# Windowed attention scored in blocks of 32 queries with 96 keys instead of 64 queries with 128 keys

## The chip, the cores and the metric

The kernel runs on one core of a Trainium2 chip. The time is the device time of one execution in microseconds (us); the runs shown are three executions of the same program, given by their median. A profile is one further execution, recorded by the hardware profiler. The engines are PE (TensorE: matmuls; PEld is its weight load), DVE (VectorE), ACT (ScalarE), POOL (GpSimd) and SP (SyncE, which here issues all DMAs).

## The reference

Sliding-window attention, then a feed-forward block with a short convolution and a gate, all in float32:

```python
B, H, S, D = 8, 8, 576, 64                      # batch, heads, sequence, head dimension
scores = q @ k.T / 8
rel = pos[:, None] - pos[None, :]
scores = where((rel >= 0) & (rel < 64), scores, -1e9)   # a query sees itself and the 63 keys before it
attn = softmax(scores); x = attn @ v            # heads laid side by side: x is [8, 576, 512]
h = relu(x @ w_in)                              # w_in 512 x 1024
conv[s] = cw[0]*h[s-1] + cw[1]*h[s] + cw[2]*h[s+1]      # zero outside the sequence
out = (h * sigmoid(conv)) @ w_out               # w_out 1024 x 512
```

## The kernel before

The 8 x 576 positions are cut into `NU` = 12 units of `NX` = 384 positions, each of `NT` = 6 tiles of `W` = 64 queries. A tile of 64 queries needs 128 keys (its own 64 and the 64 before); the first tile of a sequence has only its own 64 keys and is called narrow here (`keys_of`).

Attention of a unit is made in four batches `b` = 0..3. A batch is three tiles of four heads (two heads stand in the two halves of the 128 rows, `h`; two head pairs in the two halves of the columns, `p`). A batch passes these steps, and each is one entry of a plan:

- `qk` (L260, PE): twelve matmuls, in array tiles of 64 rows x 64 columns, write the scores into the two PSUM tiles `sc`. All batches use the same two `sc` tiles.
- `row_max` (L268, DVE): six instructions add the mask, write the scores to `s` and their row extremes to `nm`.
- `exps` (L278, ACT): six exponentials, which also sum up their rows. `reciprocal` (L281, L282, DVE).
- `normalise` (L286): scales the whole batch, on DVE in units 0 to 2, on POOL from unit 3 on.
- Transposition of the probabilities to `ub`, keys in rows: in units 0 and 1 (`BY_PE`) by PE (`transpose_pe`, L292) with a copy on ACT (`untile`, L297); from unit 2 on by DVE (`transpose`, L302), whose 32 x 32 blocks SP then puts in place by DMA (`place`, L313).

`values` (L362, PE) multiplies by v, and ACT and DVE split the result into a rounded part `xh` and a rest `xl` (L366, L369). `mm1` (L382) and `mm2` (L445) are the two large products, each as three matmuls on such split operands. Between them stand ReLU (ACT), the convolution (ACT, and DVE's L416 twice per column block), sigmoid (ACT), the gate (L428, DVE) and the split of the gated values (L432 ACT, L436 DVE).

The weights arrive as 64-bit words and are turned into float32 in the first part of the run, in sixteen pieces (eight of w_in, then eight of w_out): per piece ACT, POOL (L201), DVE (L202, L204), ACT, DVE (L208), then POOL rounds it (L217) and DVE writes the rest (L218, into `wil` or `wol`). `mm1` of column block f needs piece f of w_in, `mm2` piece f of w_out.

The order of all this is not written by hand. Each step is an entry with an engine, an assumed cost, what it reads and writes, and a due time; `queued` plays the entries through once with the assumed costs and records which it would take next on each engine. Due times of the first units stand in the table `START` (loads, weight pieces, scores, exponentials, values); the later units use fixed due times. The chip then runs each engine's instructions in that recorded order, with waits on semaphores.

Of the kernel before, what the change touches and what calls it, by code (L numbers as in the profile page):

```python
# [16 lines left out]
W = 64  # L17
B, H, S, D = 8, 8, 576, 64
# [36 lines left out]
def queued(works):  # L55
# [28 lines left out]
    while left:  # L84
        best = None
        for e, ws in waiting.items():
            if not ws:
                continue
            start = max(free[e], min(x.ready for x in ws))
            if best is None or start < best[0]:  # L90
                best = (start, e)
        start, e = best
        x = min((x for x in waiting[e] if x.ready <= start),
                key=lambda x: x.t - (0.5 if x.kind and x.kind == state[e] else 0.0))
        waiting[e].remove(x)
        turn = SWITCH[e] if e in SWITCH and (x.kind != state[e] if e == "PE" else x.kind and x.kind != state[e]) else 0.0
        if e == "PE" or x.kind:
            state[e] = x.kind
        end = free[e] = start + turn + x.cost
        if x.mb:  # L100
            dma = max(dma, end) + x.mb * 4.1
            end = dma + 1.9
        order.append(x)
        left -= 1
        for y in x.after:
            y.needs -= 1
            y.ready = max(y.ready, end + (0.0 if e == "PE" else 0.06) if y.eng == e else end + 0.2)
            if y.needs == 0:
                waiting[y.eng].append(y)
# [5 lines left out]
    "v0": -32.34,  # L115
    "pv0": -6.2,
    "conv": -32.87,
    "bits": (-33.3, -36.61, -40.93, -30.92),
    "qk1": -17.78,
    "v1": 0.96,  # L120
    "qk2": 4.55,
    "qk0": (-43.65, -39.69, -27.02, -34.75),
    "ex0": (-23.8, -21.02, -18.17, -16.66),
    "sc1": (-5.0, -10.37, -7.03, -0.86),
    "ex1": (0.34, 1.83, 2.14, 4.14),
    "in": (-23.25, -22.61, -8.35, -8.05, -5.93, -4.59, -3.56, -0.9),
    "out": (0.44, 1.55, 5.22, 5.44, 6.56, 8.03, 8.94, 11.09),
    "pv": ((4.73, 5.71, 6.92, 7.43), (5.83, 6.08, 6.48, 6.89)),
    "ex": ((5.79, 8.44, 8.97, 9.87), (6.28, 7.38, 9.35, 9.93)),
# [5 lines left out]
def attention_moe(ctx: ExitStack, tc: tile.TileContext, q, k, v, w_in, conv_w, w_out, out):  # L135
# [15 lines left out]
    mask = pool.tile([P, P], F32, name="mask")  # L151
# [4 lines left out]
    ss = many(4, [P, NB, 2, P], F32, "s")  # L156
# [38 lines left out]
    def to_f32(t, n, st, x, kb, kt):  # L195

        lw, hw, xu = st[..., 0], st[..., 1], x.bitcast(U32)
        s = n / DM

        at(t, "ACT", 0.6 * s + 0.05, lambda: nc.scalar.activation(x, hw.bitcast(F32), AF.Abs), r=[kb], w=[kt])  # L200
        at(t, "POOL", 1.45 * s + 0.15, lambda: nc.gpsimd.tensor_scalar(x, x, TINY, None, op0=ALU.max), w=[kt])  # L201
        at(t, "DVE", 0.37 * s + 0.06, lambda: nc.vector.tensor_scalar(  # L202
            xu, xu, 3, 0x3FFFFFF8, op0=ALU.logical_shift_left, op1=ALU.bitwise_and), w=[kt])
        at(t, "DVE", 0.61 * s + 0.06, lambda: nc.vector.scalar_tensor_tensor(  # L204
            xu, hw, 0xC0000000, xu, op0=ALU.bitwise_and, op1=ALU.bitwise_or), r=[kb], w=[kt])
# [27 lines left out]

    def make_masks():
        nc.gpsimd.memset(mask, 0.0)
        for h in range(2):
            mh = mask[h * W:(h + 1) * W]

            nc.gpsimd.affine_select(out=mh, in_=mh, compare_op=ALU.is_gt, fill=MASKED,
                                    base=0, pattern=[[1, P]], channel_multiplier=-1)  # L240

            nc.gpsimd.affine_select(out=mh, in_=mh, compare_op=ALU.is_ge, fill=MASKED,
                                    base=W, pattern=[[-1, P]], channel_multiplier=1)
        make_identity(nc, ident)

    def keys_of(u, t):
        return W if (u * NT + t) % SB == 0 else P  # L250

    def qk(u, b):
        g, t0 = b // 2, b % 2 * NB
        for i in range(NB):
            t = t0 + i
            n = keys_of(u, t)
            for h in range(2):
                hs = slice(h * D, (h + 1) * D)
                for p in range(2):
                    nc.tensor.matmul(sc[h][p * W:(p + 1) * W, (i + 1) * P - n:(i + 1) * P],  # L260
                                     qs[hs, 2 * g + p, t * W:(t + 1) * W],
                                     ks[hs, 2 * g + p, t * W + P - n:t * W + P], start=True, stop=True)

    def row_max(u, b):
        for i in range(NB):
            n = keys_of(u, b % 2 * NB + i)
            for h in range(2):
                nc.vector.tensor_tensor_reduce(  # L268
                    out=ss[b][:, i, h, P - n:], in0=sc[h][:, (i + 1) * P - n:(i + 1) * P], in1=mask[:, P - n:],
# [3 lines left out]
    def exps(u, b, i):  # L273
        n = keys_of(u, b % 2 * NB + i)
        for h in range(2):
            e = slice(2 * i + h, 2 * i + h + 1)
            x = ss[b][:, i, h, P - n:]
# [6 lines left out]
    def normalise(b, on):  # L284
        sv = ss[b].rearrange("p t h k -> p (t h) k")
        on.tensor_tensor(sv, sv, rs[b].unsqueeze(2).broadcast_to([P, 2 * NB, P]), ALU.mult)  # L286
# [3 lines left out]
    def transpose_pe(b, j):  # L290
        for i in range(NB):
            nc.tensor.transpose(po[b % 2 * 2 + j][:, i * P:(i + 1) * P],  # L292
                                ss[b].rearrange("p t h k -> p (t h) k")[:, NB * j + i], ident)
# [6 lines left out]
    def transpose(b):  # L300
        o = b % 2 * 2 * NB
        nc.vector.transpose(  # L302
            tbuf[:, b // 2, :, o:o + 2 * NB, :].rearrange("p j t q -> p t j q"),
            ss[b].rearrange("p t h (j q) -> p (t h) j q", q=32))
# [6 lines left out]
    def place(g, i):  # L311
        for j in range(i % 2, i % 2 + 3):
            nc.sync.dma_start(ub[g][32 * j:32 * j + 32, i], tbuf[32 * i:32 * i + 32, g, j])  # L313

    def softmax(u, qk_at, ex_at):
        for b in range(4):
            g, t = b // 2, qk_at[b]
            at(t, "PE", 0.70, lambda b=b: qk(u, b), r=[("k", g), ("q", g)], w=["sc", ("turn", b)], kind="tiled")
            for i in range(NB):
                if keys_of(u, b % 2 * NB + i) < P:  # L320
                    at(t + 0.1, "POOL", 0.2, lambda b=b, i=i: nc.gpsimd.memset(ss[b][:, i, :, :W], 0.0), w=[("s", b, i)])
            at(t + 0.17, "DVE", 1.27, lambda b=b: row_max(u, b), r=["sc", "mask"],
               w=[("s", b, i) for i in range(NB)] + [("nm", b)])
            t = ex_at[b]
            for i in range(NB):
                at(t, "ACT", 0.8, lambda b=b, i=i: exps(u, b, i), r=[("nm", b)],
# [3 lines left out]
            if u < 3:  # L330
                at(t, "DVE", 0.9, lambda b=b: normalise(b, nc.vector), r=[("r", b)], w=[("s", b, i) for i in range(NB)])
            else:
                at(t, "POOL", 1.5, lambda b=b: normalise(b, nc.gpsimd), r=[("r", b)], w=[("s", b, i) for i in range(NB)])
            t += 0.4
            sr = [("s", b, i) for i in range(NB)]
            if u < BY_PE:
                for j in range(2):
                    m = ("po", b % 2 * 2 + j)
                    at(t, "PE", 0.6, lambda b=b, j=j: transpose_pe(b, j), r=sr + ["mask"], w=[m])
                    at(t + 0.1, "ACT", 0.45, lambda b=b, j=j: untile(b, j), r=[m], w=[("u", g, i) for i in range(4)])  # L340
            else:
                t = max(t, when[-1][2] + 0.1)
                at(t, "DVE", 0.9, lambda b=b: transpose(b), r=sr, w=[("T", g)] + [("bits", i) for i in T_BITS[g]])
# [142 lines left out]
    at(-99, "POOL", 3.0, make_masks, w=["mask"])  # L486
# [111 lines left out]
```

## Time and profile before

| | |
|---|---|
| Runs shown | 543.62, 543.86, 543.85 us; median 543.85 |
| Profiled execution | 543.88 us, of which the span from first to last instruction is 542.1 |
| PE busy / PE weight loads | 510.9 us (94%) / 483.0 us (89%) |
| DVE, ACT, POOL busy | 405.6 (75%), 390.6 (72%), 122.9 us (23%) |
| Chain that ended last | PE 83%, DVE 14%, rest 3% |

How to read it: the busy shares are means over a first part, in which weights are converted and the first units' attention is made, and a long later part. The row of forty slices (13.55 us each) parts them. A matmul's recorded duration covers its way through the array, so two that follow each other overlap; the distance of their starts is what each costs. The distances below are of that kind.

### The profile page before, as it was taken

To read this page: it belongs to the slowest core of one execution; us is meant where nothing else is said; L and a number is where in the kernel's file an instruction comes from. 1 tells how busy PE (TensorE), PEld (TensorE's weight loads), DVE (VectorE), ACT (ScalarE), POOL (GpSimd) and SP (SyncE) were. 2 spreads that over 40 slices of the span, in tenths; PEclk is the share of its full clock that TensorE was granted. 3 is DMA by queue.
4 is the path that set the end of the run, shared out by engine and by line. 5 is a ranking of instruction groups with operands and counts; after the bars stand their busy time and mean duration, and the time that the engine had idled before them with its cause. 6 is when DMAs were issued, how large, how long until landed. Compare 5 with 4: busy or idle time off the path is not lost.

```text
span 542.1 us, 12584 instructions
## 1 busy us (share of the span) xinstructions
PE 510.9 (94%) x4656; PEld 483.0 (89%) x4656; DVE 405.6 (75%) x1151; ACT 390.6 (72%) x1030; POOL 122.9 (23%) x200
## 2 busy tenths in 40 slices
PE   3697598999999999999999999999999999999997
PEld 2576487999999999999999999999999999999997
DVE  2999999987767778678669677677679578575552
ACT  5798886975885885785986785786885786864441
POOL 3544665302220211212211211202211202200000
PEclk9999799999999999999999999999999999999999
DMA  8764254146154254463255262362344452030011
GB/s 337 267 255 182 91 190 160 38 130 242 27 176 136 79 140 127 137 202 108 70 173 177 57 209 53 123 171 86 129 126 125 142 160 85 19 103 2 1 58 60
DMA packets 27709, 69.83 MB, mean 129 GB/s; under 512 B 5632, under 2 KB 15360, under 8 KB 27648
## 3 DMA queue, kind: packets, MB, share of 16 engines
q1 hardware_dynamic: 27648, 69.03, 39.5%
q8 instruction: 37, 0.61, 0.5%
q14 instruction: 24, 0.20, 0.1%
HBM read 47.73 MB, written 9.47 MB: 106 GB/s over the span
## 4 chain that ended last, share of the span: by engine, by line
PE 83%; DVE 14%; issue 1%; DMA 1%; ACT 0%; SPq 0%; DVEq 0%
PE po L445 36%; PE acc L382 34%; PE sc L260 6%; PE acc L362 6%; DVE s L268 2%; DVE c L416 2%; DVE w L208 2%; DVE s L286 1%; DVE w L204 1%; DVE w L202 1%; DVE wil L218 1%; DVE wol L218 1%; DMA q<-in_q_dram 1%; DVE xl L369 1%; DVE gl L436 1%
## 5 line engine op out<-in xcount | busy, mean ns | idle before, releaser
L382 PE MATMUL acc<-xh,wih 128*128 128x384 f32 x384 | 132.7, 346 | 9.1 <-ACT hbuf L403 6.9
L445 PE MATMUL po<-gh,woh 128*128 128x386 f32 (+1 forms) x384 | 132.5, 345 | 0.4 <-POOL woh L217 0.4
L416 DVE SCALAR_TENSOR_TENSOR c<-hbuf,cw,c 128x386 f32<-128x386 f32 (+1 forms) x192 | 123.9, 693 | 10.9 <-ACT c L409 10.8
L445 PE MATMUL po<-gh,wol 128*128 128x386 f32 (+1 forms) x384 | 129.8, 338 | 1.2 <-DVE wol L218 1.2
L382 PE MATMUL acc<-xh,wil 128*128 128x384 f32 x384 | 130.5, 340 | 0.5 <-DVE wil L218 0.5
L382 PE MATMUL acc<-xl,wih 128*128 128x384 f32 x384 | 130.5, 340 | 0.0
L445 PE MATMUL po<-gl,woh 128*128 128x386 f32 (+1 forms) x384 | 129.8, 338 | 0.0
L278 ACT ACTIVATE s<-s,nm 128x128 f32<-128x128 f32 (+1 forms) x288 | 110.1, 384 | 5.6 <-DVE nm L268 5.3
L268 DVE CUSTOM_DVE_ANT_0 s<-sc,mask 128x128 f32<-128x128 f32 (+1 forms) x288 | 62.2, 277 | 33.2 <-PE sc L260 33.0
L382 PEld LDWEIGHTS acc<-xh,wih 128*128 128x128 f32 x384 | 72.7, 189 | 13.0 <-POOL w L201 7.1
L286 POOL TENSOR_TENSOR s<-s,r 128x768 f32<-128x768 f32 x36 | 54.1, 1504 | 98.2 <-DVE r L282 85.4
L445 PEld LDWEIGHTS po<-gh,woh 128*128 128x128 f32 x384 | 72.3, 188 | 4.5 <-issue 3.4
L445 PEld LDWEIGHTS po<-gh,wol 128*128 128x128 f32 x384 | 72.3, 188 | 1.8 <-DVE wol L218 1.8
L382 PEld LDWEIGHTS acc<-xh,wil 128*128 128x128 f32 x384 | 72.8, 189 | 0.8 <-DVE wil L218 0.8
L382 PEld LDWEIGHTS acc<-xl,wih 128*128 128x128 f32 x384 | 72.7, 189 | 0.0
L445 PEld LDWEIGHTS po<-gl,woh 128*128 128x128 f32 x384 | 72.3, 188 | 0.0
L436 DVE TENSOR_TENSOR gl<-c,gh 128x772 fp32r<-128x772 f32 (+1 forms) x48 | 46.0, 959 | 33.4 <-ACT gh L432 33.3
L403 ACT ACTIVATE hbuf<-acc 128x384 f32<-128x384 f32 x64 | 30.9, 486 | 45.2 <-PE acc L382 44.7
L428 DVE TENSOR_TENSOR c<-c,hbuf 128x772 f32<-128x772 f32 (+1 forms) x48 | 45.9, 956 | 22.3 <-ACT c L423 22.2
L392 POOL COPY hbuf<-hbuf 128x4 f32<-128x4 f32 x44 | 14.4, 327 | 212.5 <-DVE c L428 212.5
L423 ACT ACTIVATE c<-c 128x772 f32<-128x772 f32 (+1 forms) x48 | 40.7, 848 | 19.5 <-DVE c L416 19.2
L278 ACT ACTIVATION_READ_ACCUMULATOR s<-s,nm 128x1 f32 x288 | 54.1, 188 | 0.0
(56 smaller groups left out, 641.0 us busy)
## 6 DMA issues: line engine op xcount, KB each, us to landing
v<-in_v_dram SPq DMA_DIRECT2D x24, 768.0 KB, 4.8
ub<-T SPq DMA_DIRECT2D x240, 48.0 KB, 1.9
k<-in_k_dram SPq DMA_DIRECT2D x24, 448.0 KB, 5.5
q<-in_q_dram SPq DMA_DIRECT2D x24, 384.0 KB, 6.4
out_dram<-ot SPq DMA_DIRECT2D x8, 772.0 KB, 4.4
T<-in_w_in_dram SPq DMA_DIRECT2D x6, 512.0 KB, 6.3
T<-in_w_out_dram SPq DMA_DIRECT2D x6, 512.0 KB, 3.3
out_dram<-ot SPq DMA_DIRECT2D x3, 768.0 KB, 7.3
```

The costliest lines, as they stand in the source:

```text
L260: nc.tensor.matmul(sc[h][p * W:(p + 1) * W, (i + 1) * P - n:(i + 1) * P], qs[hs, 2 * g + p, t * W:(t + 1) * W], ks[hs, 2 * g + p, t * W + ...
L268: nc.vector.tensor_tensor_reduce(out=ss[b][:, i, h, P - n:], in0=sc[h][:, (i + 1) * P - n:(i + 1) * P], in1=mask[:, P - n:], scale=-0.125, ...
L278: nc.scalar.activation(x, x, AF.Exp, bias=nms[b][:, e], scale=-1.0, accum_out=sms[b][:, e])
L286: on.tensor_tensor(sv, sv, rs[b].unsqueeze(2).broadcast_to([P, 2 * NB, P]), ALU.mult)
L362: nc.tensor.matmul(acc[bank(("v", u, c))][h * D:(h + 1) * D, t * W:(t + 1) * W], vs[:, c, t, h], ub[g][:, 2 * p:2 * p + 2, 2 * t + h], sta ...
L382: nc.tensor.matmul(acc[bank(("m", u, f))][:, :NX], w[:, f, c], x[u % 2][:, c], start=(c == 0 and j == 0), stop=(c == NC - 1 and j == 2))
L403: nc.scalar.activation(hbuf[:, f, o:o + NX], ps[:, :NX], AF.Relu)
L416: nc.vector.scalar_tensor_tensor(c, hbuf[:, f, e:e + n], cw[:, e, f:f + 1], c, op0=ALU.mult, op1=ALU.add)
L423: nc.scalar.activation(c, c, AF.Sigmoid)
L428: nc.vector.tensor_tensor(c, c, hbuf[:, 2 * i:2 * i + 2, 1:1 + n], ALU.mult)
L436: nc.vector.tensor_tensor(gls[ring(u, i)][:, :, :n], cs[i % 2][:, :, :n], ghs[ring(u, i)][:, :, :n].bitcast(F32), ALU.subtract)
L445: nc.tensor.matmul(po[o][:, :n], w[:, f, es], x, start=(f == 0 and j == 0), stop=(f == NF - 1 and j == 2))
```

## The change

Queries are taken in blocks of `HW` = 32, each with its `KW` = 96 keys (its own 32 and the 64 before). A tile of 64 queries is two such blocks, in the two 32-row halves `s` of its 64 rows. What changes with that:

- `qk` makes 24 matmuls per batch instead of 12, in array tiles of 64 rows x 32 columns, each over 96 keys; there are no narrow tiles any more, since a second mask covers the keys before a sequence's start.
- `row_max`, `exps`, `normalise` and `transpose` work on 96 columns per tile and head instead of 128 (64 in narrow tiles). The buffers `s` are now windows in tiles `sp` that hold 32 zero columns between two blocks' probabilities; POOL writes these zeros once (`zero_pads`), and the memsets of narrow tiles (L321) go.
- `transpose_pe` becomes two ordinary matmuls with half of the identity (`iv`, 64 columns) for each former transpose, reading 128 columns of `sp` that are a block's 96 keys and 32 zeros.
- `place` issues the same twelve DMAs per half unit, at shifted offsets.
- `make_masks` issues 16 selects for two masks instead of 4 for one.
- Assumed costs and the due times in `START` are others, so the recorded order of the first units changes on every engine.

```diff
-    mask = pool.tile([P, P], F32, name="mask")
+    mask = many(2, [P, KW], F32, "mask")
-    ss = many(4, [P, NB, 2, P], F32, "s")
+    sp = many(4, [P, HW + 2 * NB * P], F32, "s")
+    ss = [x[:, HW:].rearrange("p (t h k) -> p t h k", t=NB, h=2)[:, :, :, :KW] for x in sp]
...
     def make_masks():
+        for first in range(2):
+            nc.gpsimd.memset(mask[first], 0.0)
+            for i in range(4):
+                mi = mask[first][i * HW:(i + 1) * HW]
+                nc.gpsimd.affine_select(out=mi, in_=mi, compare_op=ALU.is_gt, fill=MASKED,
+                                        base=0, pattern=[[1, KW]], channel_multiplier=-1)
+                nc.gpsimd.affine_select(out=mi, in_=mi, compare_op=ALU.is_ge, fill=MASKED,
+                                        base=W, pattern=[[-1, KW]], channel_multiplier=1)
+                if first:
+                    nc.gpsimd.memset(mi[:, :W - i % 2 * HW], MASKED)
         make_identity(nc, ident)
+    def zero_pads():
+        for x in sp:
+            nc.gpsimd.memset(x[:, :2 * NB * P].rearrange("p (e k) -> p e k", k=P)[:, :, :HW], 0.0)
+            nc.gpsimd.memset(x[:, 2 * NB * P:], 0.0)
...
     def qk(u, b):
-            t = t0 + i
-            n = keys_of(u, t)
-            for h in range(2):
-                hs = slice(h * D, (h + 1) * D)
-                for p in range(2):
-                    nc.tensor.matmul(sc[h][p * W:(p + 1) * W, (i + 1) * P - n:(i + 1) * P],
-                                     qs[hs, 2 * g + p, t * W:(t + 1) * W],
-                                     ks[hs, 2 * g + p, t * W + P - n:t * W + P], start=True, stop=True)
+            for p in range(2):
+                for s in range(2):
+                    r, t = p * W + s * HW, (t0 + i) * W + s * HW
+                    for h in range(2):
+                        hs = slice(h * D, (h + 1) * D)
+                        nc.tensor.matmul(sc[h][r:r + HW, i * KW:(i + 1) * KW], qs[hs, 2 * g + p, t:t + HW],
+                                         ks[hs, 2 * g + p, t:t + KW], start=True, stop=True)
...
     def transpose_pe(b, j):
+        iv = ident.rearrange("r (p s q) -> r s p q", s=2, q=HW)
         for i in range(NB):
-            nc.tensor.transpose(po[b % 2 * 2 + j][:, i * P:(i + 1) * P],
-                                ss[b].rearrange("p t h k -> p (t h) k")[:, NB * j + i], ident)
+            m = po[b % 2 * 2 + j][:, i * P:(i + 1) * P].rearrange("k (p s q) -> k s p q", s=2, q=HW)
+            for s in range(2):
+                o = (NB * j + i) * P + (1 - s) * HW
+                nc.tensor.matmul(m[:, s], sp[b][:, o:o + P], iv[:, s], start=True, stop=True)
...
-            dma = max(dma, end) + x.mb * 4.1
+            dma = max(dma, end) + x.mb * 2.6
-    "in": (-23.25, -22.61, -8.35, -8.05, -5.93, -4.59, -3.56, -0.9),
+    "in": (-33.517, -26.541, -25.396, -20.689, -14.772, -11.612, -10.617, -8.312),
-            at(t, "PE", 0.70, lambda b=b: qk(u, b), r=[("k", g), ("q", g)], w=["sc", ("turn", b)], kind="tiled")
+            at(t, "PE", 0.52, lambda b=b: qk(u, b), r=[("k", g), ("q", g)], w=["sc", ("turn", b)], kind="tiled")
-    at(-99, "POOL", 3.0, make_masks, w=["mask"])
+    at(-99, "POOL", 5.0, make_masks, w=["mask"])
+    at(-98, "POOL", 1.2, zero_pads, w=["pads"])
```

How the recorded order moves is seen best at three places. The first is SP's queue at the start of the program, before and then after (k, q and v are inputs, `T` and `ot` hold raw weight words, `cbits` the raw convolution weights):

```order
L183 DMA k<-in_k_dram 128x896
L184 DMA q<-in_q_dram 128x768
L183 DMA k<-in_k_dram 128x896
L184 DMA q<-in_q_dram 128x768
L214 DMA T<-in_w_in_dram 128x1024 x3
L229 DMA cbits<-in_conv_w_dram 128x48
```

```order
L218 DMA T<-in_w_in_dram 128x1024
L233 DMA cbits<-in_conv_w_dram 128x48
L187 DMA k<-in_k_dram 128x896
L188 DMA q<-in_q_dram 128x768
L187 DMA k<-in_k_dram 128x896
L188 DMA q<-in_q_dram 128x768
```

A weight piece and the small `cbits` now go out ahead of the first k and q.

The second is PE after the scores of unit 0, before and then after (`po` receives the transposes, `acc` the product with v):

```order
L292 MATMUL po_112<-ident,s_78 128x128 x3
L292 MATMUL po_113<-ident,s_78 128x128 x3
L292 MATMUL po_114<-ident,s_79 128x128 x3
L292 MATMUL po_115<-ident,s_79 128x128 x3
L362 MATMUL acc_110<-ub_61,v 64x64 x12
```

```order
L303 MATMUL po_113<-ident,s_79 128x2x32 x6
L303 MATMUL po_114<-ident,s_79 128x2x32 x6
L303 MATMUL po_115<-ident,s_80 128x2x32 x6
L303 MATMUL po_116<-ident,s_80 128x2x32 x6
```

The twelve transposes of two batches are 24 matmuls; behind them now stand the 24 score matmuls of a batch of unit 1, and only then the first product with v.

The third is DVE around the last weight piece, before and then after (`c` is the convolution, `gl` the rest of the gated values, `T` now holds transposed probabilities):

```order
L286 TENSOR_TENSOR s_81<-s_81,r_93 128x768
L208 ISA w_104<-ot,w_104 128x1024
L302 STREAM_TRANSPOSE T<-s_80 128x6x4x32
L428 TENSOR_TENSOR c_94<-c_94,hbuf 128x772
L218 TENSOR_TENSOR wol<-w_104,woh 128x512
L302 STREAM_TRANSPOSE T<-s_81 128x6x4x32
L436 TENSOR_TENSOR gl_100<-c_94,gh_97 128x772
```

```order
L293 TENSOR_TENSOR s_81<-s_81,r_93 128x6x96
L222 TENSOR_TENSOR wol<-w_105,woh 128x512
L312 STREAM_TRANSPOSE T<-s_81 128x6x3x32
L288 TENSOR_SCALAR sm_90<-sm_90 128x6
L289 RECIPROCAL r_94<-sm_90 128x6
L293 TENSOR_TENSOR s_82<-s_82,r_94 128x6x96
L436 TENSOR_TENSOR c_95<-c_95,hbuf 128x772
```

The last piece (`wol`) is now written before the last normalisation of unit 2, one transposition and the gate of the next column block, which stood ahead of it.

More of the change, by code (lines that the diff above doesn't have):

```diff
@@ L311, in place @@
     def place(g, i):
[L312 to L313 removed]
+        for j in range(3):
+            o = HW * (i % 2 + j)
+            nc.sync.dma_start(ub[g][o:o + HW, i], tbuf[HW * i:HW * (i + 1), g, j])
     def softmax(u, qk_at, ex_at):
@@ L317, in softmax @@
             g, t = b // 2, qk_at[b]
-            at(t, "PE", 0.70, lambda b=b: qk(u, b), r=[("k", g), ("q", g)], w=["sc", ("turn", b)], kind="tiled")
[L319 to L322, printed above, removed]
+            at(t, "PE", 0.52, lambda b=b: qk(u, b), r=[("k", g), ("q", g)], w=["sc", ("turn", b)], kind="tiled")
+            at(t + 0.17, "DVE", 1.1, lambda b=b: row_max(u, b), r=["sc", "mask"],
                w=[("s", b, i) for i in range(NB)] + [("nm", b)])
@@ L330, in softmax @@
             if u < 3:
-                at(t, "DVE", 0.9, lambda b=b: normalise(b, nc.vector), r=[("r", b)], w=[("s", b, i) for i in range(NB)])
+                at(t, "DVE", 0.72, lambda b=b: normalise(b, nc.vector), r=[("r", b)], w=[("s", b, i) for i in range(NB)])
             else:
-                at(t, "POOL", 1.5, lambda b=b: normalise(b, nc.gpsimd), r=[("r", b)], w=[("s", b, i) for i in range(NB)])
+                at(t, "POOL", 1.15, lambda b=b: normalise(b, nc.gpsimd), r=[("r", b)], w=[("s", b, i) for i in range(NB)])
             t += 0.4
```

60 lines of the change are left out of this document (26 added, 34 removed).

## The prediction

> **What bounds the kernel now.** I read the page first: its busy shares and forty slices.
>
> ```profile
> PE 510.9 (94%) x4656; PEld 483.0 (89%) x4656; DVE 405.6 (75%) x1151; ACT 390.6 (72%) x1030; POOL 122.9 (23%) x200
> PE   3697598999999999999999999999999999999997
> DVE  2999999987767778678669677677679578575552
> ```
>
> PE is full only from about the eighth slice on; before that DVE is. Next, the busy time by stretch (columns: length, then PE, PEld, DVE, ACT, POOL, PEclk, DMA):
>
> ```profile
> 0.00:22.00 22.00, 11.38 (x132) 8.76 (x132) 11.98 (x62) 13.48 (x52) 7.76 (x30) 1.00 0.87 336
> 22.00:97.60 75.60, 58.48 (x589) 52.10 (x589) 74.85 (x210) 63.12 (x171) 42.46 (x41) 0.95 0.47 168
> 97.60:520.00 422.40, 422.37 (x3830) 403.81 (x3831) 310.79 (x871) 307.61 (x800) 72.67 (x130) 1.00 0.38 116
> ```
>
> From 22 to 97.6 us DVE works 74.85 of 75.60 us and PE leaves 17.1 idle; from there PE has no hole at all. So the time is made of two things: when DVE has got through the weights and the first three units, and how much PE has to do from then on. The chain of waits says the same, and so does DVE's timeline at the last weight piece (last two rows), whose first reader, a block of L445, starts on PE right behind it:
>
> ```profile
> 94.82 0.87 DVE gl L436
> 95.69 1.28 DVE s L286
> 96.98 0.61 DVE wol L218
> 97.63 2.20 PE po L445 x11
> ...
> 107.16 0.68 DVE L218 TENSOR_TENSOR wol<-w,woh 128x512 fp32r<-128x512 f32 x1
> 108.11 0.34 PE L445 MATMUL po<-gh,woh 128*128 128x386 f32 x1
> ```
>
> I use that last piece as the mark, 107.8 us. The profiled execution took 543.88 us, 1.8 more than its span of 542.1, and stands at the median of the runs shown (543.85).
>
> **Scores on PE, after the mark.** A full batch, a narrow one, and what follows each:
>
> ```profile
> 144.22 0.89 PE L260 MATMUL sc<-k,q 64*64 64x128 f32 x24
> 145.04 0.44 PE L382 MATMUL acc<-xh,wih 128*128 128x384 f32 x1
> ...
> 240.12 0.78 PE L260 MATMUL sc<-k,q 64*64 64x64 f32 x24
> 240.83 0.44 PE L382 MATMUL acc<-xh,wih 128*128 128x384 f32 x1
> ...
> 144.22:144.25 0.03, 0.03 (x4) 1.00 0.00 0
> 144.25:144.38 0.13, 0.13 (x4) 1.00 0.00 0
> 144.38:144.41 0.03, 0.03 (x8) 1.00 0.00 0
> L260 PE MATMUL sc<-k,q x1152: 218/269/473, 5.2 to 454.2; 64*64 64x128 f32 x161, 64*64 64x64 f32 x31
> ```
>
> Start to start, the full batch holds PE for 0.82 us and the narrow one for 0.71. The program's 12 matmuls stand in the trace as 24 (576 as 1152), so each float32 product is two passes. The three stretch rows (length, PE busy, score matmuls in it) show four starts within 0.03 us, no new one for 0.13, then four more: the four array tiles run side by side, six rounds of them per batch. A matmul over 64 keys lasts 218 ns, one over 128 keys 269: 51 ns for 64 keys, so 96 keys save 25 ns per round. Five gaps between rounds: 5 x 0.025 = 0.13. In the last round four more tiles start, at the spacing of the four seen (0.03/4, under 8 ns), which costs what the shorter pass saves. New batch: 0.69 us, if eight tiles run side by side as four do. Bounds: all of it scaling with the keys, 0.82 x 96/128 = 0.62; or one more round, if the passes of only four tiles are laid together, 0.77. Behind the mark stand 36 batches, 12 of them with a narrow tile: 24 x 0.13 + 12 x 0.02 = 3.4 us less (bounds 5.9 and 0.5). The first 12 batches stand where PE idles and count nothing, covered by DVE's work.
>
> The Trainium skill, page "TensorE: Matmul & The Clock Gate", Part 3, gives about 4 ns for each further tile of a packed group, so eight tiles would cost 16 ns more per round than four; by it the batch is 0.70, and the sum would be the same within 0.4 us.
>
> **DVE up to the mark.** The groups by shape:
>
> ```profile
> L268 DVE CUSTOM_DVE_ANT_0 s<-sc,mask 128x128 f32<-128x128 f32 x256 | 57.6, 285 | 22.7 <-PE sc L260 22.7
> L268 DVE CUSTOM_DVE_ANT_0 s<-sc,mask 128x64 f32<-128x64 f32 x32 | 5.8, 217 | 10.4 <-PE sc L260 10.3
> L286 DVE TENSOR_TENSOR s<-s,r 128x768 f32<-128x768 f32 x12 | 12.0, 998 | 0.3
> L302 DVE STREAM_TRANSPOSE T<-s 128x768 f32<-128x768 f32 x40 | 38.8, 971 | 12.9 <-POOL s L286 8.7 <-DMA k<-in_k_dram 1.7 <-DMA q<-in_q_dram 1.7
> L428 DVE TENSOR_TENSOR c<-c,hbuf 128x772 f32<-128x772 f32 x36 | 34.5, 958 | 17.2 <-ACT c L423 17.2
> L204 DVE SCALAR_TENSOR_TENSOR w<-T,w 128x512 uint32<-128x512 uint32 x12 | 8.1, 681 | 0.1
> ```
>
> Ahead of the last weight piece the recorded order had 72 row maxima, 12 normalisations, 3 transpositions and 5 gates; now 72, 11, 2 and 4. Row maximum: (285 - 217)/2 = 34 ns less for 64 full ones, 34 ns more for 8 narrow ones: 1.9 us. Normalisation: 768 columns take 998 ns and 512 (L204) 681, so 576 save 0.24 us; 11 x 0.24 = 2.6. Transposition: the same quarter, 2 x 0.24 = 0.5. Moved behind the mark: one normalisation, one transposition, one gate and one pair of small instructions on the row sums; on the chain above, an instruction counts about 0.09 less than its duration (L436 0.87), so 0.90 + 0.88 + 0.87 + 0.3 = 2.9. Sum 7.9 us less for DVE, on the path one to one while DVE is full.
>
> **The start, which gets later.** SP's and POOL's first steps, PE's first wait and DVE's second batch:
>
> ```profile
> 0.73 0.39 SPq L183 DMA_DIRECT2D k<-in_k_dram  x1
> 1.18 0.42 SPq L184 DMA_DIRECT2D q<-in_q_dram  x1
> ...
> PE sc L260 <- DMA q<-in_q_dram: 5.2, 1, 5.2
> 1.01 0.29 POOL L239 TENSOR_SCALAR_AFFINE_SELECT mask<-mask 64x128 f32<-64x128 f32 x1
> 1.70 0.29 POOL L239 TENSOR_SCALAR_AFFINE_SELECT mask<-mask 64x128 f32<-64x128 f32 x1
> 11.96 1.49 POOL L201 TENSOR_SCALAR w<-w 128x512 f32<-128x512 f32 x1 [8.28 <-ACT w L200]
> 9.34 0.29 DVE L268 CUSTOM_DVE_ANT_0 s<-sc,mask 128x128 f32<-128x128 f32 x1 [1.44 <-PE sc L260]
> ```
>
> The first q landed at 5.2 us; now 512 KB of weights go ahead of it, at the 336 GB/s of the first stretch 1.5 us. POOL's selects come every 0.35 us (two in 0.69); 17 of them, the memsets and the zero pads keep it until about 9 us, in place of 3.6. That hides behind the late q for the mask itself (ready near 7.7). But DVE's queue now holds a step of the first weight piece (L206) right behind the first batch's row maxima; it waits for POOL's L205, which can end at 9 + 1.5 = 10.7, and the second batch's row maxima stand behind it: near 12 in place of 9.34, of which 1.5 is counted already, so 1.2 more. Bounds: nothing (DVE idles here anyway, 10 of 22 us) to 2.7; I take all 2.7, since the chain of unit 0 runs through these very steps.
>
> **Transposes on PE.** Their rows early and later:
>
> ```profile
> 15.01 1.51 PE L292 MATMUL po<-ident,s 128*128 128x128 f32 x6
> 42.43 0.49 PE L292 MATMUL po<-ident,s 128*128 128x128 f32 x3
> ```
>
> With some 0.44 and 0.27 for the last of each, the distance is 0.21 us at 15 us and 0.11 at 42. The 48 transposes stand in the trace once each; the 96 ordinary float32 matmuls should be two passes like the scores, 192. No row shows such a pass (128 stationary columns, 64 moving). Low end: half of 0.11, since half the columns move; high end: 0.21, as at 15 us. I take 0.11, as the stationary side is that of L292's row: 192 x 0.11 - 48 x 0.11 = 16 us more PE work, in the stretch where PE leaves 10.6 + 17.1 = 27.7 us idle. It fits, with some 10 us to spare, but PE and DVE now wait for each other more often; I add 1.0 (from 0, if the passes take half, to 4.7, see below).
>
> **Work moved across the mark on PE.** In the recorded order 6 matmuls of L382 more stand behind the last piece's first reader; at 0.175 (two starts in the row group of L382, or 2.10 us per 12) that is 1.05 us more.
>
> **Off the path, at nothing:** shorter exponentials on ACT and POOL's normalisation (both hidden by PE, which has no hole after 97.6 us), the memsets that go, the DMAs of `place` (same number, bytes a few less). If PE's cover were gone, DVE's and ACT's 74% load would come next.
>
> **Sum.** 542.1 - 3.4 + 1.05 - 7.9 + 2.7 + 1.0 = 535.55; with 1.8 around the span 537.3 us.
>
> **Rivals.**
> 1. *Matmuls enter no faster than now.* The quickest batch enters 24 in 0.71 us, 30 ns each. If that is an entry limit and not the length of the rounds, 48 take 1.42: 24 x 0.60 + 12 x 0.71 = 22.9 more, in place of 3.4 less: 537.3 + 26.3 = 563.6. It decides from the point where the 36 batches eat the other gains, 537.3 + 3.4 + 36 x (t - 0.78) over 543.85, t = 0.87 us or 18 ns per matmul (0.78 is the mean of 24 full and 12 narrow batches). Against it speak the stretch rows: four enter within 0.03 us. For it: no batch of the trace keeps that up beyond a round. Chance 0.12. The same page of the Trainium skill, section "Wait — 56ns, not 53.3ns?", has a floor of about 25 ns between starts however small the matmul; by that rule a batch is 1.20 us and the time 555. The four starts in 0.03 us contradict it for tiles side by side.
> 2. *The transposes hold up unit 0.* If all of unit 0's 96 passes take 0.21, they need 20.4 us against 5.1: 15.3 more, with 10.6 idle in the first 22 us to take it: 4.7 late at the least, 15.3 if none of the idle time lies at the right place. 537.3 - 1.0 + 4.7 = 541 to 552, middle 546. For it: 0.21 is the row of that place. Against: DVE is the later of the two at 30 us. Chance 0.12.
> 3. *Eight tiles don't share a round*, the change not doing what it says: 0.77 per batch, 540.2. Against it nothing in the trace, which shows no tile of 32 columns. It lies within the forecast's own range.
>
> **Chances.** The forecast (531 to 542.5, rival 3 within it) 0.72; below, if all low ends meet, 0.04; rival 1 0.12; rival 2 0.12, of which half still ends below 543. A measurement of this kernel can tell 0.2%, about 1.1 us. Faster 0.72 + 0.04 + 0.04 = 0.80; same 0.04; slower 0.12 + 0.04 = 0.16. The range: 3.4 could be 5.9, 2.7 and 1.0 could be 0, which gives 531; upward it goes into rival 2, to 548. That leaves out rival 1, the tail of rival 2 and the cases below, 0.18.
>
> **What would show it.** Batches of scores after the mark 0.69 us start to start, in six rounds of eight: right; over 0.87: rival 1. The last weight piece at 107.8 - 7.9 + 2.7 + 1.0 = 103.6 us, with DVE full from about 25 us. First score matmul near 6.7 us. L303 passes 0.11 apart and PE not full before 60 us; if DVE waits for PE between 20 and 40 us, rival 2. PE without holes after the mark; holes there, with DVE's or ACT's name, would make the sum wrong, since the new due times then starve PE.

## The result and the profile after

The changed kernel takes 549.37 us (median of 6 runs, 547.77 to 550.16), the kernel before beside it 543.95 (543.62 to 544.57): ratio 1.0095, 95% interval 1.0078 to 1.0111. It got 5.4 us slower, where 6.6 us faster was forecast, and ended outside the range of 531 to 548. The profiled execution took 549.15 us with a span of 547.4.

From the page of the changed kernel, the busy times, the slices and the shares of the chain by line:

```profile
PE 525.7 (96%) x5952; PEld 501.0 (92%) x5952; DVE 382.4 (70%) x1151; ACT 384.0 (70%) x1028; POOL 104.8 (19%) x209
...
PE   2979999999999999999999999999999999999997
...
DVE  2589989997567668668668668668668668574552
...
PE po L453 37%; PE acc L390 35%; PE sc L269 7%; PE acc L370 7%; PE po L303 4%; DMA T<-in_w_in_dram 1%; DMA q<-in_q_dram 1%; DVE c L424 1%; DVE s L276 1%; DVE w L212 1%; DVE s L293 1%; DVE w L208 0%; DVE wol L222 0%; DVE wil L222 0%; DVE c L436 0%
```

The same stretches as before (columns: length, then PE, PEld, DVE, ACT, POOL, PEclk, DMA share, GB/s):

```profile
0.00:22.00 22.00, 10.19 (x215) 8.88 (x216) 9.45 (x61) 8.88 (x34) 12.19 (x52) 1.00 0.86 325
22.00:97.60 75.60, 70.61 (x922) 66.38 (x922) 65.43 (x196) 59.13 (x172) 35.82 (x37) 0.95 0.51 172
97.60:520.00 422.40, 420.97 (x4684) 402.10 (x4683) 296.32 (x879) 306.96 (x809) 56.80 (x121) 1.00 0.36 114
```

From 22 to 97.6 us the two engines have changed places: DVE, which had worked 74.85 of 75.60 us, now works 65.43, and PE has gone from 58.48 to 70.61. What PE does more there is the transposes: start to start they hold it for 21.9 us of the stretch, where it was 6.6; its other work there got less. The groups on PE that are new or changed, and PE's first waits:

```profile
L269 PE MATMUL sc<-k,q 64*32 64x96 f32 x2304 | 43.1, 266 | 11.8 <-DMA q<-in_q_dram 8.4 <-DVE nm L276 3.4
L303 PE MATMUL po<-ident,s 128*128 128x64 f32 x192 | 27.7, 312 | 3.0 <-DVE s L293 3.0
```

L303 is busy for 27.7 us, where L292 was for 10.1 in the kernel before. The chain of waits up to 60 us (start, length, step) shows where they stand:

```profile
2.11 6.11 DMA q<-in_q_dram
...
15.80 1.39 PE sc L269 x48
17.18 10.46 PE po L303 x48
27.64 1.25 PE sc L269 x48
...
30.63 0.60 DVE w L212
31.38 7.11 DMA T<-in_w_in_dram
38.58 0.68 ACT w L204
```

Half of unit 0's transposes stand in one block of 10.4 us, 0.217 us from pass to pass. Behind them on PE's queue stands the next score batch, and behind that on DVE's queue a piece of the weights (L222), which in turn keeps a weight buffer from being loaded again (31.38). DVE's waits for scores up to the mark (total us, times, longest) have to be read with care, first those of the kernel before, then of the changed one:

```profile
DVE s L268 <- PE sc L260: 9.7, 4, 6.7
```

```profile
DVE s L276 <- PE sc L269: 16.8, 6, 9.8
```

The longest of each, 6.7 and 9.8, is the wait for the very first scores at the program's start, so it tells of the late q and not of the transposes. What the transposes do shows at 29 us, in the row maxima of the score batch behind them, again the kernel before and then the changed one:

```profile
28.95 0.23 DVE L268 CUSTOM_DVE_ANT_0 s<-sc,mask 128x64 f32<-128x64 f32 x1 [0.18 <-PE sc L260]
```

```profile
28.87 0.26 DVE L276 CUSTOM_DVE_ANT_0 s<-sc,mask 128x96 f32<-128x96 f32 x1 [3.94 <-PE sc L269]
```

From 22 to 32 us DVE works 4.4 of 10 us here, and 9.6 in the kernel before.

The last weight piece, the mark of the prediction, starts here:

```profile
L222 DVE TENSOR_TENSOR wol<-w,woh x8: 678/680/1097, 64.1 to 110.8; 128x512 fp32r<-128x512 f32 x8
```

It ends at 111.5 us (107.8 before, 103.6 forecast): 3.7 later. From there to the end are 435.9 us, against 434.3 before: 1.6 more. 3.7 + 1.6 is the whole 5.3 between the two spans.

### The profile page after: what moved, and what is told of

It is laid out like the page before. It is cut to its first block, busy times and chain, and to the rows that moved or that the text cites. A ratio compares the mean times of both kernels' runs of the same rounds, so it can differ in the third digit from the quotient of the medians.

```text
span 547.4 us, 15200 instructions
## 1 busy us (share of the span) xinstructions
PE 525.7 (96%) x5952; PEld 501.0 (92%) x5952; DVE 382.4 (70%) x1151; ACT 384.0 (70%) x1028; POOL 104.8 (19%) x209
## 4 chain that ended last, share of the span: by engine, by line
PE 89%; DVE 6%; DMA 2%; issue 1%; ACT 1%; SPq 0%; ACTq 0%; DVEq 0%
PE po L453 37%; PE acc L390 35%; PE sc L269 7%; PE acc L370 7%; PE po L303 4%; DMA T<-in_w_in_dram 1%; DMA q<-in_q_dram 1%; DVE c L424 1%; DVE s L276 1%; DVE w L212 1%; DVE s L293 1%; DVE w L208 0%; DVE wol L222 0%; DVE wil L222 0%; DVE c L436 0%
## 5 line engine op out<-in xcount | busy, mean ns | idle before, releaser
L453 PE MATMUL po<-gh,woh 128*128 128x386 f32 (+1 forms) x384 | 134.2, 349 | 0.0
L390 PE MATMUL acc<-xh,wih 128*128 128x384 f32 x384 | 131.0, 341 | 2.4 <-ACT hbuf L407 1.0
L424 DVE SCALAR_TENSOR_TENSOR c<-hbuf,cw,c 128x386 f32<-128x386 f32 (+1 forms) x192 | 119.7, 666 | 15.8 <-ACT c L417 15.4
L453 PE MATMUL po<-gh,wol 128*128 128x386 f32 (+1 forms) x384 | 129.7, 338 | 0.4 <-DVE wol L222 0.4
L453 PE MATMUL po<-gl,woh 128*128 128x386 f32 (+1 forms) x384 | 129.8, 338 | 0.0
L285 ACT ACTIVATE s<-s,nm 128x96 f32<-128x96 f32 x288 | 104.1, 364 | 5.2 <-DVE nm L276 5.0
L276 DVE CUSTOM_DVE_ANT_0 s<-sc,mask 128x96 f32<-128x96 f32 x288 | 54.9, 252 | 53.9 <-PE sc L269 53.8
L453 PEld LDWEIGHTS po<-gh,woh 128*128 128x128 f32 x384 | 72.3, 188 | 5.7
L453 PEld LDWEIGHTS po<-gh,wol 128*128 128x128 f32 x384 | 72.3, 188 | 0.7 <-DVE wol L222 0.7
L453 PEld LDWEIGHTS po<-gl,woh 128*128 128x128 f32 x384 | 72.3, 188 | 0.0
L293 POOL TENSOR_TENSOR s<-s,r 128x576 f32<-128x576 f32 x36 | 41.4, 1150 | 101.9 <-DVE r L289 85.7
L400 POOL COPY hbuf<-hbuf 128x4 f32<-128x4 f32 x44 | 11.2, 254 | 241.1 <-DVE c L436 241.1
L417 ACT ACTIVATE c<-hbuf,cw 128x386 f32<-128x386 f32 (+1 forms) x96 | 53.9, 612 | 1.4 <-DVE gl L444 1.4
L269 PE MATMUL sc<-k,q 64*32 64x96 f32 x2304 | 43.1, 266 | 11.8 <-DMA q<-in_q_dram 8.4
```

The costliest lines, as they stand in the source:

```text
L269: nc.tensor.matmul(sc[h][r:r + HW, i * KW:(i + 1) * KW], qs[hs, 2 * g + p, t:t + HW], ks[hs, 2 * g + p, t:t + KW], start=True, stop=True)
L276: nc.vector.tensor_tensor_reduce(out=ss[b][:, i, h], in0=sc[h][:, i * KW:(i + 1) * KW], in1=m, scale=-0.125, scalar=3.0e38, op0=ALU.add, o ...
L285: nc.scalar.activation(x, x, AF.Exp, bias=nms[b][:, e], scale=-1.0, accum_out=sms[b][:, e])
L390: nc.tensor.matmul(acc[bank(("m", u, f))][:, :NX], w[:, f, c], x[u % 2][:, c], start=(c == 0 and j == 0), stop=(c == NC - 1 and j == 2))
L417: nc.scalar.activation(cs[i % 2][:, a, :n], hbuf[:, f, 1:1 + n], AF.Copy, scale=cw[:, 1, f:f + 1])
L424: nc.vector.scalar_tensor_tensor(c, hbuf[:, f, e:e + n], cw[:, e, f:f + 1], c, op0=ALU.mult, op1=ALU.add)
```

## The experiments

The theory from the two traces was that the transposes on PE (twice the instructions, each two passes, in unit 0 at 0.217 us a pass) are what made the kernel slower. The rivals were the new due times, the late q, and TensorE's speed at the start as a matter of its own. All ratios are to the kernel before, run beside.

**The new blocks with the old due times**, and **the old blocks with the new due times**.

```
e1 = changed kernel,  START and x.mb * 4.1 of the kernel before
e2 = kernel before,   START and x.mb * 2.6 of the changed kernel
```

> The changed kernel with the due times in START and the assumed DMA cost of the kernel before; blocks, masks and transposes as changed. Theory A, the two-pass transposes of unit 0 hold PE and with it DVE (rows of the changed kernel: 48 passes in 10.4 us from 17.17 on): the loss stays for the most part, 545 to 549 us; only the first q comes back to 5.2 us. Theory B, the new due times themselves make the loss: the shrunk DVE work comes through and the time is 537 to 541.

> The kernel before with the changed kernel's due times and assumed DMA cost, blocks of 64 queries and one-pass transposes as before. Theory A: no long transposes here, so at most the late first q (8.4 in place of 5.2 us) costs, 543 to 547 us. Theory B: the new due times cost by themselves what the change lost, 549 us or more.

e1: 561.79 us, 1.0319 (1.0302 to 1.0337), which neither expectation had. e2: 545.12 us, 1.0017 (1.0008 to 1.0026). So the new due times are not what slowed the kernel: they cost the old blocks 1 us and save the new ones 12. e1's transposes on PE:

```profile
14.58 10.47 PE L303 MATMUL po<-ident,s 128*128 128x64 f32 x48
...
28.10 10.47 PE L303 MATMUL po<-ident,s 128*128 128x64 f32 x48 [1.57 <-DVE s L293]
```

Here both halves of unit 0's passes, 96 of them, stand 0.217 us apart, and PE waits 1.57 us for DVE ahead of the second block.

**The transposes alone, in the new blocks.** A half is turned by one `transpose` of 128 columns, in place of an ordinary matmul of 64, which is two passes; the half that isn't wanted lands in unused columns.

```
-                nc.tensor.matmul(m[:, s], sp[b][:, o:o + P], iv[:, s], start=True, stop=True)
+                nc.tensor.transpose(m[:, s, :, i::3 - i], sp[b][:, o:o + P], swapped if s else ident)
```

> The changed kernel with each half transpose made in TensorE's one-pass transpose form over all 128 columns (the unwanted half goes to unused columns of the PSUM bank): 96 passes in place of 192. Theory A: unit 0's passes take 10 us less at the slow spacing of 0.217 us, part of which comes through: 541 to 545 us. Theory B: no change of more than 1 us from the changed kernel's 549.4.

541.49 us, 0.9957 (0.9942 to 0.9972): 7.9 us less than the changed kernel, and 0.4% faster than the kernel before. (The profiled execution took 543.5 us, so the trace accounts for 5.7 of the 7.9.) Its groups, its stretch, and the last weight pieces (shortest, median and longest; first and last start):

```profile
L306 PE MATMUL po<-ident,s 128*128 128x128 f32 x48 | 13.4, 312 | 5.1 <-DVE s L297 5.1
L306 PE MATMUL po<-swapped,s 128*128 128x128 f32 x48 | 13.3, 310 | 0.0
```

```profile
22.00:97.60 75.60, 64.62 (x864) 59.76 (x863) 71.39 (x206) 61.40 (x172) 40.58 (x38) 0.95 0.51 172
```

```profile
L223 DVE TENSOR_TENSOR wol<-w,woh x8: 676/678/681, 60.8 to 105.1; 128x512 fp32r<-128x512 f32 x8
```

96 passes in place of 192; PE gives back 6 us of the stretch, DVE works 71.39 of it again, and the last weight piece ends at 105.8, 5.7 us earlier. (The two groups overlap; start to start their passes hold PE for 13.6 us, those of L303 in the changed kernel for 26.7.)

**The transposes alone, in the old blocks.**

```
 # kernel before, transpose_pe
-            nc.tensor.transpose(po..[:, i * P:(i + 1) * P], ss[b]..[:, NB * j + i], ident)
+            for s in range(2):
+                o = i * P + s * W
+                nc.tensor.matmul(po..[:, o:o + W], ss[b]..[:, NB * j + i],
+                                 ident[:, s * W:(s + 1) * W], start=True, stop=True)
```

> The kernel before (old blocks, old due times) with only the form of the transposes on TensorE changed: each as two ordinary matmuls of 64 columns, as in the changed kernel, so 192 passes in place of 48 instructions of one. Theory A (the transposes are what slowed the changed kernel; unit 0's passes stand 0.217 us apart and the chain of unit 0 runs through them): unit 0's 96 passes take some 20 us in place of 7.7, TensorE's work grows by 15 to 20 us, of which its idle time hides a part, and the time rises by 4 to 12 us, to 548 to 556 us. Theory B (they fit into TensorE's idle time ahead of the last weight piece, as the prediction had it): 544 to 545.5 us.

558.83 us, 1.0272 (1.0252 to 1.0292): 14.8 us slower, beyond even the expected range. Its chain and its group:

```profile
15.61 10.48 PE po L294 x48
28.93 10.47 PE po L294 x48
```

```profile
L294 PE MATMUL po<-ident,s 128*128 128x64 f32 x192 | 32.6, 352 | 1.5 <-DVE s L286 1.4
```

This one edit is worth more than the whole loss. The other parts of the change together, with the new due times, give 9.5 of it back (549.37 against 558.83). These parts don't simply add, though. With the old due times and the transposes in halves the new blocks are 3.0 us slower than the old ones (e1, 561.79, against 558.83); with the new due times and one-pass transposes they are 3.6 faster (541.49 against e2, 545.12). What the smaller blocks gain hangs on the due times.

**q first.** The changed kernel's SP first loads a weight piece and the convolution's weights, then k and q. Two due times were moved so that k and q go first:

```
-    "conv": -57.679,
-    "bits": (-48.434, -45.362, -58.595, -32.118),
+    "conv": -54.9,
+    "bits": (-48.434, -45.362, -55.0, -32.118),
```

> The changed kernel with the first weight piece and the convolution weights due after the first k and q, so that SP issues k, q, k, q first as in the kernel before. If the late first q (8.4 us against 5.2) is on the path: 3 us less, 546 to 547 us. If unit 0 waits for transposes and weights anyway: within 1 us of 549.4.

551.19 us, 1.0131 (1.0114 to 1.0148), 1.8 us slower than the changed kernel, which no expectation had. PE's first wait and the transposes:

```profile
L269 PE MATMUL sc<-k,q 64*32 64x96 f32 x2304 | 43.1, 266 | 9.1 <-DMA q<-in_q_dram 5.4 <-DVE nm L276 3.7
L303 PE MATMUL po<-ident,s 128*128 128x64 f32 x192 | 32.0, 345 | 2.4 <-DVE s L293 2.4
```

The first scores start 3 us earlier (5.4 for 8.4), but the transposes are busy for 32.0 us in place of 27.7, since now all 96 passes of unit 0 fall where a pass takes 0.217. The late q was not what cost the time: a gain at the start can be lost again by the speed that the transposes then meet.

**TensorE's speed.** Why do the passes stand 0.217 us apart here and 0.108 later? Matmuls of zeros were put on PE where it waits: 24 ahead of the first scores (e5), and three more behind three of unit 0's score batches (e6).

```
+    at(-199, "PE", 6.0, lambda: busy(24), r=["zeros"], w=[("po", 3)])
 # e6 as well, in softmax:
+            if u == 0 and b < 3:
+                at(t + 0.01, "PE", 0.8, lambda: busy(3), r=["zeros", "sc"], w=[("po", 3)])
```

> The changed kernel with 24 matmuls of zeros (bfloat16, 128x128 by 512) on TensorE ahead of the first scores, where it waits 8.4 us for q. Theory A (the first 48 transpose passes stand 0.217 us apart in place of 0.108 because TensorE runs at half speed after its idle start, and stays so until it has worked densely for some microseconds): the zeros bring it to full speed, the matmuls of zeros themselves fall from 0.43 to 0.21 us apart on the way, the first 48 passes take 5.2 us in place of 10.4, and the time falls by 3 to 5 us, to 544 to 546 us. Theory B (it falls back to half speed in the gaps between the four score batches that follow, whatever came before): the zeros speed up, the first transposes still take 10.4 us, time within 1 us of 549.4. Theory C (0.217 belongs to a transpose pass of 64 moving columns whose result bank is new, and has nothing to do with speed): zeros at one distance throughout, nothing gained.

> As the run before, with three more matmuls of zeros behind the first, the second and the fourth score batch of unit 0, where TensorE waits 3.4 us in all for the row maxima. Theory A: no better than the run before, or up to 1.3 us worse for the added work. Theory B: now the first 48 transpose passes take some 5.2 us and the time is 543 to 546.5 us. Theory C: 549 to 551 us.

e5: 548.07 us, 1.0088 (1.0062 to 1.0115). The zeros by stretch (length, busy, zeros in it, PEclk), then the transposes:

```profile
1.18:4.57 3.39, 3.39 (x8) 1.00 0.82 239
4.57:7.96 3.39, 3.39 (x17) 1.00 0.97 308
```

```profile
16.30 10.48 PE L304 MATMUL po<-ident,s 128*128 128x64 f32 x48
```

8 zeros take as long as the next 16 (the row's 17 counts one that began earlier): 0.427 us each, then 0.216. So TensorE does start at half speed here and doubles after 3.4 us of dense work. The Trainium skill, page "TensorE: Matmul & The Clock Gate", Part 1 ("The HAM clock gate"), has just these two rates and about 3.4 us; this row agrees. But the transposes 8 us later still take 10.4 us. The granted clock of the same trace says why (length, PE busy, then the clock and the DMA columns; first up to the last score batch, then from there through the transposes):

```profile
8.00:15.00 7.00, 3.17 (x147) 1.00 1.04 421
15.00:32.00 17.00, 17.00 (x240) 0.50 0.48 173
```

In the gaps between the score batches the clock has fallen back to half. That is theory B (though the time, 1.3 us under the changed kernel's, lies a little outside its 1 us), and C falls: the zeros' distance changes, and the slow transposes stand in a stretch of half clock. That page's rule of the Trainium skill does not fit what follows: 10.4 us of transposes without a gap did not bring the speed back, and the clock stays at 0.50 until 32 us.

e6: 545.8 us, 1.0045 (1.0010 to 1.0080), but its ten executions lie in three groups: 543.3 to 543.7 (mean granted clock 0.992 to 0.997), 545.6 to 546.2 (0.987 to 0.989) and 550.3 to 550.9 (0.978). The profile is of the last group: its block of transposes takes 10.3 us, and the granted clock is 0.50 from 17.2 to 34.2 us. What the fast ones look like was not seen. That execution times go with the mean granted clock over 7 us points to the same cause, but this is an argument, not a measurement of the block.

**Scores issued twice**, in the changed kernel (e7) and in the one before (e8):

```
-lambda b=b: qk(u, b)
+lambda b=b: (qk(u, b), qk(u, b))
```

> The changed kernel with every batch of score matmuls issued twice, so 96 passes in a row instead of 48. Theory feed (once some 32 queued pairs of weight load and matmul are used up, a pair enters every 16.7 ns): the batch grows by 48 x 16.7 = 0.80 us, from 0.76 to 1.56 us start to start, and the time by 36 x 0.80 = 29 us behind the last weight piece plus up to 12 us ahead of it: 578 to 591 us. Theory rounds (six more rounds of eight tiles at 0.082 us): the batch grows by 0.49 to 1.25 us, the time is 567 to 575 us.

> The kernel before with every batch of score matmuls issued twice, 48 passes of the old tiles (64 rows, 64 columns) in a row. Theory rounds (six more rounds of four tiles, 0.13 us by the longer keys): the batch grows by 0.65 to 0.78 us, from 0.82 to about 1.5, the time by 36 x 0.7 = 25 us and little ahead of the last weight piece: 565 to 573 us. Theory feed alone (24 more pairs at 16.7 ns): by 0.40 us, 558 to 561 us. If the old batch grows by less than the new one when both are doubled, although its matmuls have a third more keys, the new batch is bound by what feeds it.

578.03 and 572.03 us (one execution each). A batch of each and what follows it; first the changed kernel's single batch, then e7's, then e8's:

```profile
118.60 0.83 PE L269 MATMUL sc<-k,q 64*32 64x96 f32 x48
119.36 0.44 PE L453 MATMUL po<-gh,woh 128*128 128x386 f32 x1
```

```profile
201.22 1.36 PE L269 MATMUL sc<-k,q 64*32 64x96 f32 x96
202.51 0.45 PE L453 MATMUL po<-gh,woh 128*128 128x384 f32 x1
```

```profile
202.58 1.54 PE L260 MATMUL sc<-k,q 64*64 64x128 f32 x48
204.05 0.44 PE L445 MATMUL po<-gh,woh 128*128 128x384 f32 x1
```

Start to start the single batch is 0.76 us and the doubled one 1.29: 48 more passes cost 0.53, close to rounds (0.49) and far from a pair every 16.7 ns (0.80). The feed theory as a price per pass falls. But the rounds of eight are not what is seen either: behind the 33rd pass of the doubled batch one or two matmuls start every 16.7 ns, to its end. The old batch grows from 0.82 to 1.47, 0.65, as expected by rounds. The time of e7 alone would have spoken for feed; its last weight piece tells why:

```profile
L222 DVE TENSOR_TENSOR wol<-w,woh x8: 676/678/684, 71.3 to 120.1; 128x512 fp32r<-128x512 f32 x8
```

It ends at 120.8, 9.3 us later than in the changed kernel, and from there to the end are 455.4 us, 19.5 more: 36 batches at 0.54. The doubled batches ahead of the mark cost time too, so the time as a whole doesn't tell the two theories apart.

**The batch in two steps**, 16 matmuls and 8, other matmuls between (with the one-pass transposes). In unit 3 the exponentials of two batches then come ahead of their scores, and a unit's last batch may read the next unit's q and k; the amount of work is the same.

```
+                at(t, "PE", 0.36, lambda b=b: qk(u, b, (0, 1)), ..., kind="tiled")
+                at(t + 0.7, "PE", 0.18, lambda b=b: qk(u, b, (2,)), ..., w=["sc"], kind="scores")
```

> The one-pass transposes in the new blocks, with each score batch from unit 2 on in two steps of TensorE, 16 matmuls (two tiles of the batch) and 8 (the third) a while later, so that other matmuls can come between. Theory queue (the first 33 or so passes of a run of scores go in rounds of eight 0.082 us apart, because they stand queued; those behind them come one by one): a piece of 16 matmuls, 32 passes, takes 4 x 0.082 and the turn, about 0.46 us, a piece of 8 about 0.30, none shows the tail of starts 16.7 ns apart, and a whole batch in two pieces costs about the same as one of 0.76, since the turn is paid twice. Theory tile (the third tile of a batch is slow for itself, by its place in the bank): the piece of 8 shows starts 16.7 ns apart and takes 0.4 us or more. The time itself, with due times not tuned for it: 541 to 548 us.

551.78 us (one execution), above the 541 to 548 expected. A piece of 32 passes, and one of 16:

```profile
209.56 0.56 PE L274 MATMUL sc<-k,q 64*32 64x96 f32 x32
210.05 0.45 PE L462 MATMUL po<-gh,woh 128*128 128x386 f32 x1
...
229.38 0.40 PE L274 MATMUL sc<-k,q 64*32 64x96 f32 x16
229.70 0.44 PE L462 MATMUL po<-gh,woh 128*128 128x386 f32 x1
```

0.49 and 0.32 us: two rounds of eight more cost 0.165, 0.082 each, as four rounds of a batch do. At that pace a whole batch would be 0.32 + 4 x 0.082 = 0.65 us; it takes 0.76, so the last 16 passes of 48 cost 0.11 more than rounds would. The third tile alone (0.32) doesn't show it, so it is not the tile but its place behind 32 others. The single starts in the changed kernel's trace fit: up to about the 33rd pass of a batch they come in rounds, then mostly one every 16.7 ns. What limits them was not settled. Splitting does not pay: 0.81 for 0.76.

**The best of both**: one-pass transposes with 20 + 9 matmuls of zeros.

> The one-pass transposes in the new blocks (541.5 us), with 20 matmuls of zeros ahead of the first scores and three behind each of the first, the second and the fourth score batch of unit 0. Theory A (what is left to gain is TensorE's half speed in unit 0's transposes, and dense work ahead of them brings it up in part of the executions): 539 to 541 us, spread over some 5 us from execution to execution. Theory B (the transposes stay at 0.213 us a pass whatever goes ahead; the zeros only delay): 541.5 to 543 us.

540.61 us (539.32 to 541.41), 0.9934 (0.9916 to 0.9953): 0.66% faster than the kernel before, the fastest here. Its first transposes now run at full speed (two starts 0.11 us apart), a later half, after a wait, at half:

```profile
18.55 0.27 PE L307 MATMUL po<-ident,s 128*128 128x128 f32 x1
18.66 0.27 PE L307 MATMUL po<-swapped,s 128*128 128x128 f32 x1
...
31.36 0.45 PE L307 MATMUL po<-ident,s 128*128 128x128 f32 x1 [2.87 <-DVE s L298]
31.59 0.42 PE L307 MATMUL po<-swapped,s 128*128 128x128 f32 x1
```

Its interval overlaps that of the one-pass transposes without zeros; that the zeros gain anything is not shown.

## Why the prediction was wrong

- **Transposes on PE, +1.0: the step that failed.** The count (192 passes) was right. The price was not: 0.11 was taken for all of them, where the row at 15 us had shown 0.21; the first half of unit 0's 96 passes holds PE for 10.4 us and the second, from 33.27 to 40.67 less 1.5 of waiting, for 5.9 us, 16.3 and not 10.6; all 192 for 26.7 and not 21. And the larger part: "It fits" added up 27.7 us of idle time over 98 us, though a block of passes can only use the idle time where it stands: PE takes its work in the recorded order, so next scores, DVE's row maxima and the weight pieces behind those on DVE's queue all stood behind it. In the old blocks this part alone measured +14.8 us (e9), and taking half of the passes away gave 7.9 us back (e3). The sum had put the mark at 103.6; it came 7.9 later, which is two thirds of the 11.8 us by which the span missed the sum. The other 3.9 lie behind the mark (below).
- **Rival 2 is what happened**, though only half of unit 0's passes took 0.21. That 549.4 lies inside its 541 to 552 is in part luck, since the rest of that sum was too low by the 3.9 us behind the mark. Its sign came (between 20 and 40 us DVE waits 3.9 us for PE's scores, 0.2 in the kernel before), and "DVE is the later of the two at 30 us", held against it, was a state of the kernel before that the longer block itself removed. It had 0.12; the row at 15 us deserved more.
- **DVE up to the mark, -7.9: right as work, wrong as time.** DVE's busy time up to the mark went from 96.96 us (of 107.8) to 88.67 (of 111.5), 8.3 less. "One to one while DVE is full" did not hold, since DVE was no longer full (2589989997 in the slices): the saving became waiting (rows up to the mark, the kernel before and then the changed one).

```profile
0.00:107.80 107.80, 80.03 (x779) 71.03 (x780) 96.96 (x288) 85.78 (x245) 53.02 (x75) 0.97 0.52 191
```

```profile
0.00:111.50 111.50, 93.96 (x1207) 87.78 (x1207) 88.67 (x283) 80.82 (x240) 50.88 (x93) 0.97 0.52 184
```

- **The start, +2.7: about right.** q landed at 8.2 us, not 6.7, but the second batch's row maxima came at 12.3 (near 12 forecast, from a start that was 1.5 too early), and the first transpose at 17.2 in place of 15.0. Moving q forward did not help (e4), since the transposes then got slower.
- **Scores after the mark, -3.4: mis-sized.** A batch is 0.76, not 0.69: start to start the 36 batches take 27.4 us against 28.2, 0.8 less. Eight tiles do share a round, 6.7 ns from tile to tile, rounds 0.082 apart from the second on, but the last third of a batch doesn't keep the rounds. Rival 1 is wrong (16 ns per pass, and no batch behind the mark over 0.87). The Trainium skill, page "TensorE: Matmul & The Clock Gate", section "Wait — 56ns, not 53.3ns?", states a floor of about 25 ns between starts. It doesn't hold for these tiles, and the 555 us by it fall with it: eight matmuls enter in 0.08 us.

```profile
204.31:204.39 0.08, 0.07 (x8) 1.00 1.09 403
```

- **Moved across the mark, +1.05: right** (5 matmuls and 1.0 us). What is left of the 1.6 is 0.65 us of idle time behind the mark, which the prediction had at nothing, and 0.6 on L453.
- "No row shows such a pass" was true of the form, but a row did show the place (0.21 at 15 us), and the place decided the price.

## What to carry to other kernels

Work put "into the idle time" of an engine has to be laid at the place in the queue where it will stand: price it with the row nearest in time, then ask what stands behind it in order and who waits for that. When an edit takes work from the engine that bounds a stretch and adds some to the one that had slack, compare the two after the edit; here 8 us less on DVE turned into waiting for transposes that hold PE for 26.7 us, where they had held it for 9.6. A transpose in float32 was dearer here as an ordinary matmul, which is two passes, than as a transpose, even where the latter moved twice the columns: at the start 0.43 us against 0.21.

## What the runs showed of the hardware

- A pass of 64 columns as an ordinary float32 matmul and one of 128 as a transpose both stand 0.21 us apart at the start and 0.11 (0.108 and 0.102) later.
- In both kernels TensorE runs at half speed until some 30 us: a score batch at 27.6 us takes 1.14 us start to start, the one at 30 us 0.76 (1.28 and 0.82 in the kernel before).
- The granted clock tells which only from its first change on. The changed kernel inside the block of transposes, and at its second half:

```profile
22.00:26.00 4.00, 4.00 (x21) 4.00 (x20) 1.29 (x2) 2.65 (x10) 1.01 (x1) 1.00 0.12 48
34.00:36.00 2.00, 2.00 (x20) 1.99 (x18) 2.00 (x15) 1.52 (x3) 2.00 (x2) 1.00 0.94 320
```

At 1.00 in both, as many passes take 4 us in the one and 2 in the other. The first clock record of this trace begins at 29.9 us, and a stretch without a record reads 1.00; there the distance from start to start has to be read instead. Behind the first record the two agree, as in the last kernel (transposes 0.11 apart, then 0.21):

```profile
17.40:28.20 10.80, 4.25 (x35) 1.00 0.67 228
31.36:33.90 2.54, 2.54 (x12) 0.50 0.86 346
```

- Full speed came after 3.4 us of dense bfloat16 matmuls, did not come in 10.4 us of transposes, and was kept by transposes once it was there (17.4 to 28.2 us in the last kernel). It ended there in a wait of 2.87 us (clock 0.50 from 31.2 us), but a wait of the same length did not end it in the one-pass kernel (30.7 to 33.6 us, clock 1.00). The clock records between two changes are all 3.41 us long or a multiple of it (3.4, 6.8, 10.2, 17.1 and longer in these traces); what decides inside one was not tested.
